# A new order for the layer norm stage: first tile transposed into two PSUM tiles, second tile's statistics begun with the other half

## The chip, the cores and the metric

The kernel runs on one core of a Trainium2 chip. The metric is the device time of one execution in microseconds (us); the time of the kernel before is the median of three runs. PE is the matmul engine, PEld its weight loads, DVE the vector engine, ACT the scalar engine, POOL the general-purpose engine, and SP issues most of the transfers.

## The reference

The input x has 2048 tokens of 512 values. It is normalised per token (`xn = (x - mean) / sqrt(var + eps)`), and two branches read xn; their sum and x are the output.

```python
xn = _layernorm(x)
return x + _A_ref(xn, A_wqkv, A_wo) + _B_ref(xn, B_w_in, B_w_sp, B_b_sp, B_w_out)
# _A_ref: q, k, v = xn @ wqkv, 32 heads of 16; each token attends to itself and
#         7 earlier tokens at a distance of 2, 4 ... 14; then @ wo
# _B_ref: z = gelu(xn @ w_in), 2 x 688 columns; z2 = layernorm(second half)
#         g = w_sp @ z2 + b_sp;  (z1 * g) @ w_out
```

## The kernel before, in words

The 2048 tokens are 16 tiles of 128. A tile has a place `tb` (0 to 3) and a block `j` (0 to 3); its number is `4 * tb + j`, and a block is the four tiles of one `j`. All matmuls need xn with its 512 values along the partitions, so each tile goes through the same chain: load (L167 in halves for the first two tiles of block 0, L175 for the others), statistics on DVE (`bn_stats`, L213 and L217, `bn_aggr`, L220), reciprocal root on ACT (L223) or, for block 3, on POOL (L226, L227), apply in place on DVE (L231), and a transpose into `xnT`. Block 0 and the first two tiles of block 1 are transposed by PE (L238, L248) into a PSUM tile `pt`, which ACT (L242, L252) or DVE (L253) copies to `xnT`; the other ten tiles by a DMA transpose that SP issues (L257).

What follows the chain closely: the q columns of block 0 are multiplied tile by tile as its transposes arrive (`q_tile`, L327, matmuls of 128 columns), the k columns and those of block 1 as matmuls of 512 or 256 columns (`qk_part`, L321), and ACT copies the results out of PSUM (`qk_copy`, L337). Then come the z matmuls of branch B (`zmm`, L263), whose left operands are `xnT` tiles of blocks 1 and 2, and DVE's products q times k (L361).

Five engines have a manual schedule: every engine executes its instructions in the order in which the program writes them, and waits in that order. Up to the first z matmul this order is written out as calls (L597 to L699). After that it is a list of tokens, `ORDER`, that a loop at L724 turns into calls: `z1.3` is the z matmul of tile `j=1, tb=3`, and so on.

PSUM buffers come from two pools: `ps_mm` with three buffers of two banks, `ps_aux` with two of one bank. A tile of a pool waits until the tile that last had the buffer has been read.

Ahead of the first data PE runs ten matmuls on a tile of zeros (`warm_up(10)`), and two short ones between the transposes of the first two tiles and the first q matmul. The second tile of block 0 arrives in two halves, one issued by SP (`h=0`), one by ACT (`h=1`). `ln_stats(i, 2)` reads them in the order 0, 1:

```python
for n in range(2):
    ln_stats(t0[n], 2)
    ln_root(col(t0[n]))
for n in range(2):
    ln_apply(t0[n])
pts = [tr(t0[n]) for n in range(2)]
tr_copy(t0[0], pts[0], 0, 2)
tr_copy(t0[0], pts[0], 2, 4)
tr_copy(t0[1], pts[1], 0, 2)
warm_up(2, 1)
```

Of the kernel before, what the change touches and what calls it, by code (L numbers as in the profile page):

```python
# [7 lines left out]
BF16 = mybir.dt.bfloat16  # L8
F32 = mybir.dt.float32
# [5 lines left out]
P = 128  # L15
# [24 lines left out]
CHUNKS = (1, 1, 1, 1, 1, 1, 1, 1)  # L40
ORDER = """
z1.3 z2.0 z1.2 z2.2 zg1.3 p0.1 zg2.0 zg1.2 q2.2 zg2.2 p0.3 zs2.2 q2.3 p1.2 qc2.2 p1.3 q2.1 qc2.3 p1.0
z1.0 p0.2 qc2.1 w3 z2.1 p0.0 zg1.0 zs1.0 q2.0 p2.2 zg2.1 a1 z2.3 qc2.0 w2 zg2.3 p2.3 halo zs2.0 z3.0 p2.0 z1.1
w0 zg3.0 b1 z0.1 zg1.1 p2.1 zs2.3 X0 a0 zg0.1 z3.2 Xg0 zs1.1 z3.3 a2 zg3.2 z3.1 zs1.2 zg3.3 z0.2 b0 zg3.1 X4
b2 zg0.2 zs3.3 L0 L1 Xg4 q3.1 p3.2 zs3.1 p3.0 Lc0 q3.0 Lc1 p3.1 qc3.1 q3.2 p3.3 qc3.0 zs0.1 a3 z0.3 qc3.2 q3.3
zg0.3 p4.1 zs1.3 p4.0 z0.0 qc3.3 X1 p4.2 zg0.0 zs0.3 X2 p4.3 Xg1 X5 st.0 zs2.1 st.1 a4 Xg2 L2 V6 zs0.2 zs3.2
b3 Xg5 V2 b4 Vc6 zs0.0 p5.3 L3 V5 zs3.0 p5.2 Vc2 V1 st.2 p5.1 Vc5 p5.0 V0 st.3 a5 w4 Lc2 Vc1 V4 st.4 Vc0 w1
N1.1 V3 N2.0 Vc4 N1.0 b5 Lc3 V7 N0.0 Vc3 M0.0 N1.2 M0.1 L5 N0.2 L4 Vc7 N3.3 X6 N0.1 M0.2 N0.3 late X3 N3.1
N1.3 N2.1 G0.0 N2.2 Xg6 N2.3 N3.2 N3.0 G0.1 p7.1 G0.2 M0.3 G0.3 p7.2 G4 p6.0 Gi0 w6 Lc4 p6.3 Xg3 p6.2 E0 p7.3
G3 p6.1 U0 S0.0 p7.0 a6 w9 G1 Gi3 Gi4 S0.1 b6 a7 G2 Gi1 w7 U1 S0.2 b7 S0.3 w5 S0.4 Lc5 R0 L6 L7 G6 Lc6 A0 Gi2  # L50
Lc7 U2 U4 mask T4 U3 M1.0 A1 T2 G7 A2 Gi6 w8 A3 wo1.2 A4 T0 A5 X7 M1.1 Gi7 A6 wo1.3 xr0 G5 A7 Xg7 A8 w10 M1.2
A9 w12 U7 A10 X8 Gi5 A11 X10 T1 A12 G8 Xg10 A13 Xg8 wo1.0 A14 T7 M1.3 A15 G9 Gi8 A16 A17 E1 A18 A19 wo0.2
wo0.3 G10 wo0.1 U6 wo1.1 U5 Gi9 wo0.0 A20 T3 S1.0 S1.1 A21 X9 S1.2 G12 A22 S1.3 Gi10 T5 A23 S1.4 T6 A24 Xg9
w15 A25 X15 A26 Gi12 w14 X12 R1 Xg15 X11 A27 Xg12 w11 A28 O0 Xg11 A29 A30 A31 Or0 O1 A32 A33 A34 Or1 U8 Oh0.0
A35 A36 Oh0.1 Fe0.0 A37 Fe0.1 A38 G14 Fe0.2 Fe0.3 F0.2 F0.0 F0.1 s0.0 A39 s0.1 F0.3 A40 xr1 A41 Oh1.0 w13 A42
U10 Oh1.1 Fe1.0 U9 T8 Gi14 A43 Fe1.1 A44 T10 X13 A45 G11 s0.2 T9 A46 s0.3 F1.0 A47 A48 G13 F1.1 Gi11 s1.1 Xg13
U11 U12 Fe1.2 A49 T12 A50 A51 X14 A52 G15 Xg14 Fe1.3 U14 Gi13 F1.3 F1.2 A53 s1.2 T11 A54 T14 A55 O2 Gi15 s1.0
A56 U15 U13 T15 A57 Or2 xr2 Oh2.0 A58 A59 s1.3 Oh2.1 T13 Fe2.0 Fe2.1 xr3 F2.0 O3 Fe2.2 Fe2.3 F2.2 F2.1 s2.0
s2.2 F2.3 s2.1 s2.3 Or3 Of Oh3.1 end
# [10 lines left out]
def kernel(  # L70
# [98 lines left out]
    def load_wqk(E, s):  # L169
        for kc in range(C):  # L170
            E.dma_start(wqk[:, s, kc], A_wqkv[kc * P:(kc + 1) * P, s * D:(s + 1) * D])

    def load_x(E, j, b0, b1):
        for tb in range(b0, b1):
            E.dma_start(xall[:, j, tb], xblk[j][:, tb])  # L175
# [4 lines left out]
    load_x(A, 0, 2, 4)  # L180
    load_wqk(SP, 0)
    load_x(SP, 1, 0, 2)
    load_wqk(SP, 1)
    load_x(SP, 1, 2, 4)
    load_x(SP, 2, 0, 4)
# [23 lines left out]
    def ln_stats(i, parts=1):  # L209
        j, tb = i % 4, i // 4  # L210
        w = D // parts
        for h in range(parts):
            V.bn_stats(stats[:, i, 6 * h:6 * h + 6], xall[:, j, tb, w * h:w * h + w])  # L213
        ln_agg(i, parts)

    def ln_bn(i):
        V.bn_stats(stats[:, i, 0:6], xall[:, i % 4, i // 4, :])  # L217

    def ln_agg(i, parts=1):
        V.bn_aggr(mv[:, i, :], stats[:, i, 0:6 * parts])  # L220

    def ln_root(sl):
        A.activation(rstd[:, sl], mv[:, sl, 1], ACT.Abs_reciprocal_sqrt, bias=eps_t[:])  # L223

    def ln_root_pool(i):
        G.tensor_tensor(rstd[:, i:i + 1], mv[:, i, 1:2], eps_t[:], ALU.add)  # L226
        G.tensor_tensor(rstd[:, i:i + 1], rstd[:, i:i + 1], mhalf[:], ALU.pow)  # L227

    def ln_apply(i):
        j, tb = i % 4, i // 4  # L230
        V.tensor_scalar(xall[:, j, tb, :], xall[:, j, tb, :], mv[:, i, 0:1], rstd[:, i:i + 1],  # L231
                        ALU.subtract, ALU.mult)

    def tr(i):
        j, tb = i % 4, i // 4
        pt = ps_aux.tile([P, C, P], BF16, name="pt", tag="aux")
        for c in range(C):
            PE.transpose(pt[:, c, :], xall[:, j, tb, c * P:(c + 1) * P], ident[:])  # L238
        return pt

    def tr_copy(i, pt, c0=0, c1=C):
        A.copy(xnT[:, c0:c1, i * P:(i + 1) * P], pt[:, c0:c1, :])  # L242

    def tr2(i):
        j, tb = i % 4, i // 4
        pts = [ps_aux.tile([P, 2, P], BF16, name="pt", tag="aux") for _ in range(2)]
        for c in range(C):
            PE.transpose(pts[c // 2][:, c % 2, :], xall[:, j, tb, c * P:(c + 1) * P], ident[:])  # L248
        return pts

    def tr_copy2(i, pts):
        A.copy(xnT[:, 0:2, i * P:(i + 1) * P], pts[0][:])  # L252
        V.tensor_copy(xnT[:, 2:4, i * P:(i + 1) * P], pts[1][:])  # L253

    def tr_dma(i):
        j, tb = i % 4, i // 4
        SP.dma_start_transpose(xnT[:, :, i * P:(i + 1) * P], xall[:, j, tb, :])  # L257
# [66 lines left out]
    def q_tile(tb, kcs):  # L324
        for kc in kcs:
            for c in range(C):
                PE.matmul(pqs[c // 2][:, c % 2, tb * P:(tb + 1) * P], wqk[:, 0, kc, c:D:C],  # L327
                          xnT[:, kc, 4 * tb * P:(4 * tb + 1) * P], start=(kc == 0 and tb % 2 == 0), stop=(kc == C - 1 and tb % 2 == 1))
# [252 lines left out]
    def blk(j):  # L581
        return [4 * tb + j for tb in range(TB)]

    def col(i):
        return slice(i, i + 1)

    def blk_cols(j):
        return slice(j, NT, 4)

# [4 lines left out]

    t0, i1 = blk(0), blk(1)
    i2, i3 = blk(2), blk(3)
    warm_up(10)  # L597
    for n in range(2):
        ln_stats(t0[n], 2)
        ln_root(col(t0[n]))  # L600
    for n in range(2):
        ln_apply(t0[n])
    pts = [tr(t0[n]) for n in range(2)]
    tr_copy(t0[0], pts[0], 0, 2)
    tr_copy(t0[0], pts[0], 2, 4)
    tr_copy(t0[1], pts[1], 0, 2)
    warm_up(2, 1)
    pqs = [qk_tile() for _ in range(3)]
    ln_stats(t0[2])
    ln_root(col(t0[2]))  # L610
    tr_copy(t0[1], pts[1], 2, 4)
    q_tile(0, (0, 1))
    q_tile(0, (2,))
    q_tile(1, (0, 1))
    q_tile(0, (3,))
    ln_bn(t0[3])
    ln_apply(t0[2])
    ln_agg(t0[3])
    pt2 = tr2(t0[2])
    q_tile(1, (2, 3))  # L620
    ln_root(col(t0[3]))
    tr_copy2(t0[2], pt2)
    ln_apply(t0[3])
    q_tile(2, (0, 1))
    pt3 = tr2(t0[3])
    q_tile(2, (2, 3))
    tr_copy2(t0[3], pt3)
    q_tile(3, (0, 1))
    q_tile(3, (2, 3))
    ln_stats(i1[0])  # L630
    ln_root(col(i1[0]))
    qk_copy(pqs[0], 0, 0)
    ln_stats(i1[1])
    ln_root(col(i1[1]))
    qk_part(pqs[2], 0, 2, 0, 4, (0,))
    ln_apply(i1[0])
    qk_part(pqs[2], 0, 2, 0, 4, (1,), kcs=range(2))
    pt = tr(i1[0])
    qk_part(pqs[2], 0, 2, 0, 4, (1,), kcs=range(2, 4))
    ln_stats(i1[2])  # L640
    qk_copy(pqs[1], 0, 1)
    ln_root(col(i1[2]))
    ln_apply(i1[1])
    tr_copy(i1[0], pt)
    ln_bn(i1[3])
    ln_apply(i1[2])
    tr_dma(i1[2])
    ln_agg(i1[3])
    pq3 = qk_tile()
    qk_part(pq3, 0, 3, 0, 4, (0,), kcs=range(2))  # L650
    pt = tr(i1[1])
    qk_part(pq3, 0, 3, 0, 4, (0,), kcs=range(2, 4))
    tr_copy(i1[1], pt)
    ln_root(col(i1[3]))
    ln_apply(i1[3])
    tr_dma(i1[3])
    load_x(SP, 3, 0, 4)
    qk_part(pq3, 0, 3, 0, 4, (1,))
    qk_copy(pqs[2], 0, 2)
    qk_copy(pq3, 0, 3)  # L660
    for n in range(4):
        ln_stats(i2[n])
    ln_root(slice(2, 7, 4))
    ln_root(slice(10, 15, 4))
    A.preload_act_table_set("gelu_apprx_tanh_and_others")
    table[0] = "gelu"
    for i in i2:
        ln_apply(i)
        tr_dma(i)
    for n in range(3):  # L670
        ln_stats(i3[n])
        ln_root_pool(i3[n])
    ln_apply(i3[0])
    tr_dma(i3[0])
    ln_stats(i3[3])
    ln_root_pool(i3[3])
    for i in i3[1:3]:
        ln_apply(i)
        tr_dma(i)
    pqs = [qk_tile() for _ in range(3)]  # L680
    for c in range(3):
        qk_part(pqs[c], 1, c, 0, 2)
    pa3 = ps_aux.tile([P, 2, 2 * P], F32, name="pa3", tag="aux")
    qk_part(pa3, 1, 3, 0, 2)
    qk_copy(pa3, 1, 3, 0, 2)
    for c in range(3):
# [70 lines left out]
```

## Time and profile before

| | |
|---|---|
| median of 3 runs | 202.04 us (201.27 to 202.22) |
| profiled execution, first to last instruction | 199.94 us |
| what lies around it: median less that span | 2.10 us |
| PE busy | 195.4 us, 98% |
| DVE busy | 184.6 us, 92% |
| ACT busy | 103.9 us, 52% |
| moved by DMA | 25.91 MB, mean 130 GB/s |
| mean granted TensorE clock | 1.000 |

A profile is one execution. A row of its groups or timeline names the line of the kernel, the engine, the operation, the tile written and the tile read; what stands in brackets is the engine's idle time ahead of it and what ended it. The chain of waits is followed back from the last instruction to whatever released each step. [...]

### The profile page before, as it was taken

What the parts mean: (1) busy time and instruction counts of PE and PEld (TensorE: products, weight loads), DVE (VectorE), ACT (ScalarE), POOL (GpSimd) and SP (SyncE); (2) the same over time, 40 slices, a digit from 0 to 9 for tenths busy, and PEclk for the clock granted to TensorE, in tenths of its full rate; (3) what the DMA queues carried; (4) which work ended last, traced back from release to release, by engine and by line L of the source; (5) the groups of instructions that cost most, each with busy time, mean ns of one, the idle gap of its engine ahead of it and who ended that gap; (6) DMA issues with size and microseconds to landing.
All of it is one profiled execution on the core that took longest, in us unless ns stands there. A gap on an engine that the chain in (4) does not pass through costs nothing.

```text
span 199.9 us, 4102 instructions
## 1 busy us (share of the span) xinstructions
PE 195.4 (98%) x1691; PEld 123.9 (62%) x1691; DVE 184.6 (92%) x249; ACT 103.9 (52%) x175; POOL 22.0 (11%) x23
## 2 busy tenths in 40 slices
PE   7899999999999999999999999999999999999994
PEld 2869756665566666666656666666544646664562
DVE  5789899999999999999979999999999999999624
ACT  3586978899899976453431523708402230331400
POOL 3000800699500000000000000000000000000000
DMA  5986548950000096524477999199940297219863
GB/s 160 266 244 163 106 78 240 234 113 3 0 0 3 3 157 115 167 64 100 61 152 161 239 220 192 49 217 180 192 85 0 81 208 169 72 32 127 215 209 105
DMA packets 66562, 25.91 MB, mean 130 GB/s; under 512 B 56496, under 2 KB 66288, under 8 KB 66288
## 3 DMA queue, kind: packets, MB, share of 16 engines
q1 hardware_dynamic: 65824, 25.18, 58.4%
q10 hardware_dynamic: 720, 0.48, 0.8%
q8 instruction: 13, 0.21, 0.4%
q14 instruction: 5, 0.04, 0.1%
HBM read 10.13 MB, written 2.10 MB: 61 GB/s over the span
## 4 chain that ended last, share of the span: by engine, by line
PE 95%; DMA 1%; DVE 1%; SPq 0%; ACT 0%; issue 0%
PE pg L470 37%; PE pz L263 19%; PE pq L321 11%; PE pv L431 7%; PE po L553 7%; PE po L523 6%; PE pa L553 2%; PE pq L327 2%; DMA r_x<-in_A_x_dram 1%; PE pl L381 1%; PE pa L321 1%; PE po L532 1%; PE pb L523 1%; PE pt L238 0%; DVE r_pr L541 0%; DVE stats L213 0%
## 5 line engine op out<-in xcount | busy, mean ns | idle before, releaser
L470 PE MATMUL pg<-z,r_qk 128*128 128x344 bf16 x448 | 66.8, 309 | 0.0
L470 PEld LDWEIGHTS <-r_qk 128*128 128x128 bf16 x448 | 43.8, 98 | 22.0 <-issue 0.4
L445 DVE TENSOR_TENSOR r_pr<-r_x,r_w 128x2048 bf16<-128x2048 bf16 x32 | 38.4, 1220 | 1.3 <-PE pl L381 1.0
L263 PE MATMUL pz<-w_z,xnT 128*128 128x344 bf16 x256 | 39.3, 309 | 0.0
L449 DVE TENSOR_TENSOR r_pr<-r_pr 128x2048 bf16<-128x2048 bf16 x28 | 33.9, 1219 | 0.4
L263 PEld LDWEIGHTS <-xnT 128*128 128x128 bf16 x256 | 25.0, 98 | 13.2 <-issue 0.4
L476 ACT ACTIVATE gs<-pg,b_col 128x688 bf16<-128x688 f32 x16 | 13.2, 834 | 35.4 <-PE pg L470 26.4
L361 DVE TENSOR_TENSOR r_pr<-r_qk 128x2048 bf16<-128x2048 bf16 x24 | 27.9, 1222 | 0.2 <-ACT r_qk L337 0.2
L321 PE MATMUL pq<-xnT,r_w 128*128 128x512 bf16 (+1 forms) x128 | 23.8, 339 | 0.0
L321 PEld LDWEIGHTS <-r_w 128*128 128x128 bf16 x144 | 15.9, 114 | 7.6 <-issue 0.4
L536 ACT CAST r_qk<-po 128x512 bf16<-128x512 f32 x10 | 5.5, 588 | 22.7 <-PE po L553 22.7
L699 POOL CAST b_col<-b 128x16 f32<-128x16 bf16 x1 | 15.7, 15704 | 11.8 <-DMA b<-in_B_b_sp_dram 11.8
L337 ACT CAST r_qk<-pq 128x1024 bf16<-128x1024 f32 x15 | 14.9, 1015 | 2.4 <-PE pq L321 2.3
L312 ACT ACTIVATE r_uz<-pz 128x688 bf16<-128x688 f32 x16 | 11.7, 740 | 6.6 <-PE pz L263 6.5
L523 PE MATMUL po<-r_lg,r_pr 32*128 32x512 bf16 x192 | 14.5, 375 | 0.0
L431 PE MATMUL pv<-xnT,r_w 128*32 128x512 bf16 x256 | 14.2, 379 | 0.0
L553 PEld LDWEIGHTS <-r_uz 128*128 128x128 bf16 x85 | 8.0, 98 | 9.5 <-issue 1.1
L370 DVE TENSOR_TENSOR r_pr<-r_pr 128x4096 bf16<-128x4096 bf16 x6 | 13.7, 2289 | 0.0
L553 PE MATMUL po<-r_w,r_uz 128*128 128x512 bf16 x60 | 13.6, 380 | 0.0
L281 ACT ACTIVATE z<-pz 128x688 bf16<-128x688 f32 x16 | 11.9, 744 | 1.5 <-PE pz L263 1.5
L287 ACT ACTIVATE junk<-z 128x688 bf16<-128x688 bf16 x16 | 12.4, 774 | 0.1
L431 PEld LDWEIGHTS <-r_w 128*32 128x32 bf16 x256 | 9.5, 138 | 4.3
(88 smaller groups left out, 200.3 us busy)
## 6 DMA issues: line engine op xcount, KB each, us to landing
r_lg<-in_A_wo_dram SPq DMA_DIRECT2D x8, 256.0 KB, 4.2
r_x<-in_A_x_dram SPq DMA_DIRECT2D x12, 128.0 KB, 3.0
out_dram<-r_qk SPq DMA_DIRECT2D x12, 128.0 KB, 2.1
r_w<-in_A_wqkv_dram SPq DMA_DIRECT2D x8, 128.0 KB, 3.6
r_qk<-in_A_x_dram SPq DMA_DIRECT2D x8, 128.0 KB, 2.2
w_z<-in_B_w_in_dram SPq DMA_DIRECT2D x4, 172.0 KB, 4.4
w_z<-in_B_w_in_dram SPq DMA_DIRECT2D x1, 688.0 KB, 5.5
r_w<-in_B_w_out_dram SPq DMA_DIRECT2D x1, 640.0 KB, 6.5
```

The costliest lines, as they stand in the source:

```text
L263: PE.matmul(pz[:, hh, 0:FHALF], xnT[:, kc, i * P:(i + 1) * P], wz[:, kc, hh * FHALF:(hh + 1) * FHALF], start=(kc == 0), stop=(kc == C - 1))
L321: PE.matmul(pq[:, cc, p0 * P:(p0 + b1 - b0) * P], wqk[:, sd, kc, c0 + cc:D:C], xv[:, kc, b0:b1, j, :], start=(kc == 0), stop=(kc == C - 1))
L337: cast = A.copy(dst, pq[:, :, p0 * P:(p0 + b1 - b0) * P].rearrange("p c (b t) -> p c b t", b=b1 - b0))
L361: prod = V.tensor_tensor(pr[g % 3][:, c].rearrange("p w b t -> p b w t"), q3.unsqueeze(2).broadcast_to([P, TB, 4, P]), k4, ALU.mult)
L370: V.tensor_tensor(pr[g % 3][:, 0:2], pr[g % 3][:, 0:2], pr[g % 3][:, 2:4], ALU.add)
L431: PE.matmul(pv[32 * tb:32 * tb + 32, dd, :], wv[:, kc, 2 * d2 + dd, :], xnT[:, kc, tb * TBS:(tb + 1) * TBS], start=(kc == 0), stop=(kc == ...
L445: V.tensor_tensor(pw_t[n], vp[:, :, off:off + P], a_sb[:, slot_w(w), ts].unsqueeze(1).broadcast_to([P, DH, P]), ALU.mult)
L449: V.tensor_tensor(pw_t[n] if dst is None else dst, pw_t[n], pw_t[m], ALU.add)
L470: PE.matmul(pg[:, hh, 0:FHALF], wsp[n][:, k, :], z2[:, k, hh * FHALF:(hh + 1) * FHALF], start=(k == 0), stop=(k == NT - 1))
L523: PE.matmul(pc, op[32 * tb:32 * tb + 32, d, o * P:(o + 1) * P], wo_r[32 * tb:32 * tb + 32, d, cs], start=(d == 8), stop=False, tile_positi ...
L553: mm = PE.matmul(pc, uT[:, o % 2, m, tb * P:(tb + 1) * P], wout[:, m, cs], start=False, stop=(m == MCH - 3))
L699: G.tensor_copy(b_col[:], b16[:])
```

## The change

The calls that wrote out the first stage become tokens of a second list, `START`, ahead of `ORDER`; the first tokens of `ORDER` move to its end, and the rest is the same text. The loads are the same transfers in the same order on the same queues; the last block's tiles are loaded in the order 0, 1, 3, 2. In the new order:

- The second tile's statistics read half 1 (ACT's) and then half 0 (SP's): `ls0.1.1 ls0.1.0`.
- The two short warm-up matmuls stand ahead of the first transposes.
- The first tile's four transposes go into two `ps_aux` tiles of two each (`lt0.0.0.2 lt0.0.2.4`), the second tile's into one large tile of `ps_mm` (`lt0.1.0.4.1`).
- The q matmuls run tile 0 to its end, then the first half of tile 1, where before they alternated.
- The third tile's two copies are both ACT's; the fourth tile is transposed after one quarter of the third tile's q matmuls instead of two.
- In block 1 the statistics of tile 3 come ahead of tile 2, and one copy of a whole tile goes to DVE (`lc1.1.0.4.1`).
- In block 2 the statistics of the second tile come first, and the DMA transposes go out as tiles 0, 1, 3, 2. Those of block 3 go out as 3, 0, 2, 1.
- Some of the k matmuls of block 0 stand in another order around the transposes of block 1.

No matmul, activation or statistics is added or removed.

```diff
+START = """
+warm10.4 ls0.0.0 ls0.0.1 la0.0 lr0.0 ls0.1.1 ls0.1.0 la0.1 lr0.1 ln0.0 ln0.1 warm2.1 lt0.0.0.2 lt0.0.2.4 lt0.1.0.4.1 lc0.0.0.2 lc0.0.2.4 lc0.1.0.2 ls0.2 la0.2 lr0.2 lc0.1.2.4 qt0.0 qt0.1 qt0.2 qt0.3 qt1.0 qt1.1 ls0.3 ln0.2 la0.3 lr0.3 lt0.2.0.2 lt0.2.2.4 ln0.3 lc0.2.0.2 lc0.2.2.4 qt1.2 qt1.3 qt2.0 lt0.3.0.2 lc0.3.0.2 lt0.3.2.4 qt2.1 qt2.2 qt2.3 qt3.0 ls1.0 lc0.3.2.4.1 qt3.1 qt3.2 qt3.3 la1.0 lr1.0 c0 ls1.1 la1.1 lr1.1 ln1.0 km2.1.0.2 km2.0.0.4 km2.1.2.4 lt1.0 km3.0.0.2 ls1.3 ls1.2 la1.2 c1 lr1.2 ln1.1 lt1.1 lc1.0.0.4 ln1.2 ld1.2 la1.3 km3.0.2.4 lr1.3 lc1.1.0.4.1 ls2.1 ln1.3 ld1.3 lx3.0.1 lx3.1.2 lx3.3.4 km3.1.0.4 y0.0 c2 c3 ls2.0 la2.0 la2.1 lr2.0.2 ln2.0 lx3.2.3 ld2.0 ls2.2 ls2.3 la2.2 la2.3 lr2.2.2 ln2.1 ln2.3 ld2.1 ld2.3 ls3.0 la3.0 lp3.0 ls3.1 la3.1 lp3.1 ln2.2 ls3.2 ld2.2 la3.2 lp3.2 ls3.3 la3.3 lp3.3 ln3.0 ln3.1 ln3.2 y1.0 y2.0 y3.0 gelu yc3.0 y0.1 yc0 y1.1 y2.1 yc1 y3.1 yc2 yc3.1 p1.1 ln3.3 ld3.3 ld3.0 ld3.2 ld3.1 lv lz lb z1.3 z2.0 z1.2 z2.2 zg1.3 p0.1 zg2.0 zg1.2 q2.2 zg2.2 p0.3 zs2.2 q2.3 p1.2 qc2.2 p1.3 q2.1 qc2.3 p1.0 z1.0 p0.2 qc2.1 w3 z2.1 p0.0 zg1.0 zs1.0 q2.0 p2.2 zg2.1 a1 z2.3 qc2.0 w2 zg2.3 p2.3 halo zs2.0 z3.0 p2.0 z1.1 w0 zg3.0 b1 z0.1 zg1.1 p2.1 zs2.3 X0 a0 zg0.1 z3.2 Xg0 zs1.1 z3.3 a2 zg3.2 z3.1 zs1.2 zg3.3 z0.2 b0 zg3.1 X4 b2 zg0.2 zs3.3
+"""
...
+    def ln_stats(j, tb, h=None):
+        i = 4 * tb + j
+        if h is None:
+            V.bn_stats(stats[:, i, 0:6], xall[:, j, tb, :])
+        else:
+            halves.add(i)
+            V.bn_stats(stats[:, i, 6 * h:6 * h + 6], xall[:, j, tb, 256 * h:256 * h + 256])
...
+    def tr(j, tb, c0=0, c1=C, big=0):
+        if big:
+            pt = ps_mm.tile([P, 16, P], BF16, name="pt", tag="mm")
+        else:
+            pt = ps_aux.tile([P, c1 - c0, P], BF16, name="pt", tag="aux")
+        for c in range(c0, c1):
+            pts[j, tb, c] = pt, c0
+            PE.transpose(pt[:, c - c0, :], xall[:, j, tb, c * P:(c + 1) * P], ident[:])
+
+    def tr_copy(j, tb, c0, c1, on_dve=0):
+        i = 4 * tb + j
+        pt, o = pts[j, tb, c0]
+        (V.tensor_copy if on_dve else A.copy)(xnT[:, c0:c1, i * P:(i + 1) * P], pt[:, c0 - o:c1 - o, :])
...
+    def qk_step(sd, ms, tb, kc):
+        for m in ms:
+            for cc in range(2):
+                PE.matmul(p0[m][:, cc, tb * P:(tb + 1) * P], wqk[:, sd, kc, 2 * (m % 2) + cc:D:C],
+                          xnT[:, kc, 4 * tb * P:(4 * tb + 1) * P], start=(kc == 0 and tb % 2 == 0),
+                          stop=(kc == C - 1 and tb % 2 == 1))
...
+    steps = {"warm": warm_up, "ls": ln_stats, "la": ln_agg, "lr": ln_root, "lp": ln_root_pool, "ln": ln_apply, "lt": tr,
+             "lc": tr_copy, "ld": tr_dma, "qt": q_step, "kt": k_step, "kk": k3_step, "km": k_wide, "qw": q_pair, "kp": k_pair, "nb": ln_shift, "c": c0_copy, "y": y_part, "yt": y_tile, "yc": y_copy,
+             "lx": lambda j, b0, b1: load_x(SP, j, b0, b1), "lw": load_z2, "lv": load_v, "lz": load_z1, "lb": load_b,
...
+    for tok in START.split() + ORDER.split():
```

In a token the first number after the name is the block and the second the tile's place in it (`ls` statistics, `la` aggregate, `lr` and `lp` root on ACT and POOL, `ln` apply, `lt` transposes on PE with the range of the four 128-value pieces, `lc` copy, `ld` DMA transpose, `qt` q matmuls of one tile and one piece, `km` k matmuls of block 0, `y` q and k matmuls of block 1, `c` and `yc` their copies).

## Prediction

> **What bounds the kernel now.** I read the page first: PE is busy for 98% of the span and makes up 95% of the chain that ended last.
>
> ```profile
> PE 195.4 (98%) x1691; PEld 123.9 (62%) x1691; DVE 184.6 (92%) x249; ACT 103.9 (52%) x175; POOL 22.0 (11%) x23
> ...
> PE 95%; DMA 1%; DVE 1%; SPq 0%; ACT 0%; issue 0%
> ```
>
> A busy PE may hide short stalls, so I took the start times of successive matmuls next. Those of 128 columns start 56 ns apart, 512 columns 216 ns, 344 columns 146 ns. From 6.03 us until the last one at 196.91 us only two starts come later than that without a change of form: 0.065 us each, at 8.48 and 9.66 us. So behind 6.03 us there are 0.13 us to win on PE, and everything else must come from starting earlier. The chain of waits up to 30 us, in order of time, shows what sets that start (start, length, what):
>
> ```profile
> 1.25 2.92 DMA r_x<-in_A_x_dram
> 4.17 0.02 issue
> 4.20 0.76 DVE stats L213 x2
> 4.96 0.02 issue
> 4.98 0.22 DVE mv L220
> 5.20 0.02 issue
> 5.23 0.30 ACT rstd L223
> 5.53 0.03 issue
> 5.56 0.42 DVE r_x L231
> 5.98 0.05 issue
> 6.03 0.40 PE pt L238 x4
> 6.42 0.11 PE pwm L592 x2
> 6.53 1.35 PE pq L327 x24
> ```
>
> The end hangs on one transfer: the half of the second token tile that SP issued at 1.25 us and that is whole at 4.17 us. Statistics, aggregate, root, apply and transpose follow without slack. The timeline says the same from the engines' side:
>
> ```profile
> 5.53 0.90 PE L238 MATMUL pt<-ident,r_x 128*128 128x128 bf16 x8 [0.60 <-DVE r_x L231]
> ...
> 5.96 0.92 ACT L242 COPY xnT<-pt 128x256 bf16<-128x256 bf16 x3 [0.44 <-PE pt L238]
> ...
> 7.28 0.40 DVE L231 TENSOR_SCALAR r_x<-r_x,mv,rstd 128x512 bf16<-128x512 bf16 x1
> ```
>
> **Statistics of the second tile.** The landing events of the trace say when each transfer was whole: SP's half at 4.17 us, ACT's half at 3.99 us. The kernel before reads SP's half first, so DVE, which could take a new instruction at about 3.95 us, stands until 4.20. The changed order reads ACT's half at 3.99 + 0.02 = 4.02 us; its successor starts 0.34 us later, at 4.36, when the other half has long landed. The aggregate moves from 4.98 to 4.80 us, **0.18 us earlier**. DVE then runs on without a wait, so apply, root and statistics of the next tiles all move by 0.18: the first apply to 4.93, the second to 5.38, the third tile's apply from 7.28 to 7.10 us.
>
> **The first tile in two PSUM tiles.** Its first copy now waits for two transposes instead of four. A transpose shows 0.219 us from start to end and a copy starts 0.037 us behind (5.922 to 5.959), so two fewer starts bring the copy 0.11 us forward: with the apply's 0.18 it starts at 5.67 and ends at 6.04. The two short warm-up matmuls, 0.11 us in the chain, move ahead of the transposes into PE's idle time. The first q matmul needs the second tile's transposes issued (apply ends 5.79, they start at 5.85, four times 0.056: 6.08) and the copy (6.04 + 0.05), so it starts at 6.09 instead of 6.38, 0.29 earlier. But that lead isn't kept. Twenty-four q matmuls take 1.34 us (to 7.43; the fourth quarter of the q weights, whole at 6.80 us, holds them back by about 0.09 to 7.52), and then the third tile's transposes wait for its apply: 7.10 + 0.40 + 0.06 = 7.56 instead of 7.74. So 0.11 of the 0.29 is lost to a new wait, and **the split itself is worth nothing here**; its cover is DVE's chain.
>
> **Tiles three and four.** Tile three's second copy moves from DVE to ACT (0.29 and 0.37 us there), which lets DVE apply tile four at 7.96 instead of 8.38. The q matmuls on tile three still wait for the copy after its transposes (8.30 for 8.48). The other wait of 0.065 us, at 9.66, goes: tile four's transposes now stand four q matmuls earlier, its copy ends at 9.21, and PE comes at 9.41. **Gain 0.065 us.**
>
> **Blocks one to three.** PE is then 0.25 us early at its first 512-column matmul (10.31 for 10.55). What could stop it:
> - The second tile of block one is transposed at 12.69; its apply ends, by the DVE rows (landing of the last quarter of the block at 10.78, two statistics of 0.68 and 0.66, aggregate 0.18, apply 0.38), at 12.58. That leaves 0.05 us after the 0.06 that the transpose lags. This cover is thin, because the tile that lands last is now measured first.
> - One 128x512 copy leaves ACT (0.59 us) for DVE, ahead of a matmul that needs it at 14.2 us; by two copies of 0.29 it ends near 13.7. On ACT the two later q copies end near 14.4 and 15.4; PE needs them at 15.1 and 15.9 (now 0.28 and 0.23 us to spare).
> - SP issues the same loads in the same order. Its transposes of block one follow the applies: 13.15 and 14.60 us, now 13.62 and 15.03. What is queued behind moves by 0.43: the eight transposes from 18.38 to about 17.95.
> - The wait on POOL's root (0.44 us of DVE before its second product) sits behind 24 us and costs PE nothing.
>
> No instruction is added or removed on PE, so behind this stage the 0.25 us stay. DVE, which also starts its products about 0.25 earlier (22.85 for 23.12), keeps its distance.
>
> **Sum.** 0.18 + 0.065 = 0.245 us off the profiled execution's 199.94 us span: 199.69. The runs shown have a median of 202.04 us, 2.10 above that span (launch and end, and the spread of executions); less 0.25, **201.8 us**. The unknown costs, from both sides: if the third apply did not hold PE, the gain would be 0.36; if SP's half lands first, the 0.18 is gone.
>
> **Rivals.**
> 1. *No gain.* The lead of ACT's half is 0.18 us in one execution, on DMA engines that are 80% busy from 2 to 4 us and 92% from 4 to 6. If it flips, DVE waits for the later half in the changed order as it does now, and 0.07 us remain; a last quarter of block one late by 0.2 us costs 0.15. Then 202.0 us.
> 2. *Slower: a stall at the z matmuls (L263) of block two.* The transposes of block two now go out as tiles 0, 1, 3, 2, and PE needs tile 2 before tile 3. At 1.3 us apiece tile 2 is issued at 21.86 and lands at 24.33 us (fourth place: 22.29 to 24.76 before); PE comes at 24.94 - 0.25 = 24.70. It decides from a landing 0.36 us late. The row that speaks for it: of the sixteen landing events of the transfer now in fourth place, fifteen lie by 24.76 and one at 25.86, 1.10 late, beside an instruction fetch at 24.50; PE then needed it at 25.96. A repeat would land at 25.43: stall 0.73, net +0.5, so 202.5 us. The next one was late by 2.12 us (27.33, 29.45) beside a fetch of 1.47 us; that would stall 1.75 and give 203.5 us. Against it: such fetches are few, eighteen in the span by the page's rows and four of them between 11 and 30 us, and the place is earlier by 0.43 us.
>
> ```profile
> q8 instruction: 13, 0.21, 0.4%
> q14 instruction: 5, 0.04, 0.1%
> ```
>
> 3. *Faster by over 1 us*, if executions that I have not seen hold stalls in this stage that the new order avoids (tile 3 of block two, with 0.11 us to spare in the profile, now goes third): about 200.9 us.
>
> [...]
>
> That the change doesn't do what it says I rule out: in the program, each of the first three copies has its own wait on PE, and the second tile's first statistics wait on ACT's transfer.
>
> **Chances.** Forecast 0.57, no gain 0.15, stall of a good half microsecond 0.13, stall of 1.5 us or more 0.08, faster by over 1 us 0.07. About 0.5%, 1.0 us, is what a measurement of this kernel tells from no change (its runs spread over 201.27 to 202.22). The first three cases lie within it: faster 0.07, same 0.85, slower 0.08. The range goes from the fastest run less the largest gain (201.27 - 0.36 = 200.9) to the slowest with the smaller stall and some of the flip (202.22 + 0.5 + 0.1 = 202.8).
>
> **What would show it.** Right: second tile's statistics start near 4.02 us, first q matmul near 6.1, third tile's transposes near 7.56, the first 512-column matmul near 10.31, the z matmuls of block two without a gap, span 199.7. Wrong: the statistics start at 4.2 again (rival 1), or matmuls on block two's tile 2 start behind a gap near 24.7 (rival 2), or PE has gaps near 12.7.

## The result, and the profile after

The changed kernel takes **202.71 us** (median of 11 runs, 201.69 to 203.33) where the kernel before takes 201.68 us (median of 11 runs, 201.27 to 202.22). The ratio is 1.0042 with a 95% interval of 1.0027 to 1.0057: slower, by less than 0.5%, where 0.1% faster was forecast.

The runs of the changed kernel lie in two groups. With the twelve of the first experiment there are 23: nine from 201.35 to 202.06 us (mean 201.79) and fourteen from 202.45 to 203.33 (mean 202.87). So two questions stand: what the 1.1 us are that fourteen of 23 runs pay, and why the other nine are no faster than before.

The profiled execution took 201.77 us, so it belongs to the lower group: span 200.1 us, 0.1 more than the 199.94 of before (unrounded, 200.05). From its page, busy time and the chain by engine, with matmuls now on L259 (z), L317 and L325 (q, k), transposes on L244:

```profile
PE 196.1 (98%) x1691; PEld 124.3 (62%) x1691; DVE 184.7 (92%) x249; ACT 103.9 (52%) x175; POOL 5.6 (3%) x23
...
PE 98%; DVE 0%; ACT 0%; issue 0%
```

The chain of waits (start, length, what) no longer begins with a transfer:

```profile
1.04 4.66 PE pwm L642 x12
5.71 0.23 PE pt L244 x2
5.93 0.02 issue
5.95 0.38 ACT xnT L249
6.33 0.04 issue
6.38 1.69 PE pq L325 x24
8.07 0.22 PE pt L244 x4
...
10.81 1.73 PE pq L317 x8
```

On DVE the times came out as forecast: in its timeline the second tile's statistics start at 3.96 us (4.20 before) and the third tile's apply at 7.10, as forecast. But the first q matmul starts at 6.38 as before, not at 6.09, because PE itself was late: the clock rose only at 5.78 us in this execution, the transposes went 107 ns apart, and the twelve warm-up matmuls ahead of them filled PE's time. Then the 24 q matmuls take 0.19 us longer than before, because they wait for the third and the fourth quarter of the q weights (whole, by the last of their landing events, at 6.86 and 7.16 us; 6.41 and 6.80 before), and 0.08 of that comes back at tile four. So the first 512-column matmul starts at 10.65 us (10.55 before), and what follows keeps that distance to the end. PE's timeline shows the four z products without a break, before and after (24.70 was forecast for the fourth; it starts at 25.03):

```profile
21.44 4.83 PE L263 MATMUL pz<-w_z,xnT 128*128 128x344 bf16 x32
```

```profile
21.53 4.83 PE L259 MATMUL pz<-w_z,xnT 128*128 128x344 bf16 x32
```

So this one execution of the lower group shows why it isn't faster than before. It holds nothing of the upper group; that took another profile.

### The profile page after: what moved, and what is told of

It reads as the page before. It is cut to its first block, busy times and chain, and to the rows that moved or that the text cites. A ratio compares the mean times of both kernels' runs of the same rounds, so it can differ in the third digit from the quotient of the medians.

```text
span 200.1 us, 4105 instructions
## 1 busy us (share of the span) xinstructions
PE 196.1 (98%) x1691; PEld 124.3 (62%) x1691; DVE 184.7 (92%) x249; ACT 103.9 (52%) x175; POOL 5.6 (3%) x23
## 4 chain that ended last, share of the span: by engine, by line
PE 98%; DVE 0%; ACT 0%; issue 0%
PE pg L529 37%; PE pz L259 19%; PE pq L317 11%; PE pv L490 7%; PE po L612 7%; PE po L582 6%; PE pwm L642 2%; PE pq L325 2%; PE pa L612 2%; PE pl L440 1%; PE pa L317 1%; PE po L591 1%; PE pb L582 1%; PE pt L244 1%; DVE r_pr L600 0%; ACT xnT L249 0%
## 5 line engine op out<-in xcount | busy, mean ns | idle before, releaser
L259 PE MATMUL pz<-w_z,xnT 128*128 128x344 bf16 x256 | 39.3, 310 | 0.0
L259 PEld LDWEIGHTS <-xnT 128*128 128x128 bf16 x256 | 24.9, 98 | 13.2 <-issue 0.4
L317 PE MATMUL pq<-xnT,r_w 128*128 128x512 bf16 (+1 forms) x128 | 23.8, 340 | 0.0
L317 PEld LDWEIGHTS <-r_w 128*128 128x128 bf16 x144 | 15.9, 114 | 7.6 <-issue 0.4
L582 PEld LDWEIGHTS <-r_pr 32*128 32x128 bf16 x272 | 7.5, 93 | 6.7 <-issue 1.0
```

The lines of the kernel that those rows point to most:

```text
L259: PE.matmul(pz[:, hh, 0:FHALF], xnT[:, kc, i * P:(i + 1) * P], wz[:, kc, hh * FHALF:(hh + 1) * FHALF], start=(kc == 0), stop=(kc == C - 1))
L317: PE.matmul(pq[:, cc, p0 * P:(p0 + b1 - b0) * P], wqk[:, sd, kc, c0 + cc:D:C], xv[:, kc, b0:b1, j, :], start=(kc == 0), stop=(kc == C - 1))
L582: PE.matmul(pc, op[32 * tb:32 * tb + 32, d, o * P:(o + 1) * P], wo_r[32 * tb:32 * tb + 32, d, cs], start=(d == 8), stop=False, tile_positi ...
```

## The experiments

**e1: the changed kernel again**, for a second profile.

> The changed kernel once more, for a second profile and more times. Its eleven times lie in two groups, 201.7 to 201.9 us (three, the profiled one among them) and 202.4 to 203.3 us (eight). Late landing (the second rival of the prediction): in the upper group the DMA transpose of block two's tile 2, now fourth, lands about 1 us late, and a profile of that group shows a gap of 0.7 to 1.1 us on PE near 24.8 us. Late clock: in the upper group PE's clock comes up later than the 5.8 us of the profile shown, and a profile of that group shows q matmuls 107 ns apart instead of 56 for some microseconds behind 6 us, and no gap at 24.8. Both expect a ratio near 1.004.

Measured: 202.27 us (12 runs), ratio 1.0031 (1.0013 to 1.0049). Its profiled execution took 203.19 us, one of the upper group, although the clock rose early, at 4.28 us. A late clock is therefore not what the upper group pays for. PE's timeline, and the chain that led to the broken place:

```profile
21.77 3.66 PE L259 MATMUL pz<-w_z,xnT 128*128 128x344 bf16 x24
26.46 1.34 PE L259 MATMUL pz<-w_z,xnT 128*128 128x344 bf16 x8 [1.03 <-DMA xnT<-r_x]
```

```profile
22.92 0.09 DVE r_x L233
23.02 3.40 DMA xnT<-r_x
26.42 0.05 issue
26.46 1.34 PE pz L259 x8
```

Eight of the 32 z matmuls, those on tile 2 of block two, stand behind a DMA transpose issued at 23.02 us that took 3.40 us to land. Start to start, PE loses 1.20 us there: about 0.93 because the landing is that much later than the 2.47 us that a transpose in time takes, 0.22 because the transpose was issued too late for PE even so, and 0.05 from landing to start. That is the second rival's place.

**e2 to e4: which edit makes it.** e2 puts only block two's transposes back in the order 0, 1, 2, 3, e3 only the two short warm-ups; e4 gives the kernel before only the new order of transposes.

```diff
# e2, in START
-ln2.1 ln2.3 ld2.1 ld2.3
+ln2.1 ln2.2 ld2.1 ld2.2
...
-ln2.2 ls3.2 ld2.2
+ln2.3 ls3.2 ld2.3
# e3, in START
-ln0.1 warm2.1 lt0.0.0.2
+ln0.1 lt0.0.0.2
...
-lc0.1.0.2 ls0.2
+lc0.1.0.2 warm2.1 ls0.2
# e4, in the kernel before
-    for i in i2:
+    for i in (i2[0], i2[1], i2[3], i2[2]):
         ln_apply(i)
         tr_dma(i)
```

> The changed kernel with the DMA transposes of block two (and the applies ahead of them) in the order 0, 1, 2, 3 again. Late landing: PE gets tile 2 from the third place, 1.3 us earlier, the upper group goes, the ratio falls to about 0.999. Late clock: the first 10 us are untouched, so the ratio stays near 1.004 and the two groups stay.

> The changed kernel with the two short warm-up matmuls back between the transposes and the q matmuls. Late landing: nothing changes, ratio near 1.004 (the two matmuls cost 0.1 us at most). Late clock: if the place of these two matmuls decides when the clock comes up, the upper group goes or shrinks and the ratio falls towards 1.000.

> The kernel before with one part of the change alone: DMA transposes of block two in the order 0, 1, 3, 2. Late landing: the same upper group appears, ratio 1.002 to 1.005. Late clock: same as before within 0.1%.

| | median us | ratio (95%) | PE gap at the fourth z product |
|---|---|---|---|
| e2 | 201.87 (201.79 to 202.31) | 1.0013 (1.0005 to 1.0022) | none |
| e3 | 202.95 (202.55 to 203.49) | 1.0063 (1.0049 to 1.0077) | 0.91 us |
| e4 | 202.38 (202.27 to 202.48) | 1.0034 (1.0021 to 1.0047) | 0.67 us |

e2 removes the upper group (its clock rose at 6.98 us, the latest of all), e4 makes it out of the kernel before. PE's timeline of e2, then of e4:

```profile
21.62 4.83 PE L259 MATMUL pz<-w_z,xnT 128*128 128x344 bf16 x32
```

```profile
21.41 3.66 PE L263 MATMUL pz<-w_z,xnT 128*128 128x344 bf16 x24
25.58 1.34 PE L263 MATMUL pz<-w_z,xnT 128*128 128x344 bf16 x8 [0.50 <-DMA xnT<-r_x]
```

The bracket gives less than the gap from start to start (0.50 for 0.67 us in e4), since a matmul's end is modelled. All five runs of e4 lie between 202.27 and 202.48 us. e3 shows that the place of the warm-ups isn't the cause. Its ratio lies above e1's: all six of its runs are in the upper group, of e1's six of twelve, and no row shows why.

**e5 to e8: where the lead of 0.25 us went.** On e2, whose profile has no stall: e5 puts the old order of the first 24 q matmuls back, e6 the old order of the second tile's halves, e7 the first tile's transposes in one PSUM tile. e8 gives the kernel before the new order of q matmuls.

```diff
# e5
-qt0.0 qt0.1 qt0.2 qt0.3 qt1.0 qt1.1
+qt0.0 qt0.1 qt0.2 qt1.0 qt1.1 qt0.3
# e6
-ls0.1.1 ls0.1.0
+ls0.1.0 ls0.1.1
# e7
-lt0.0.0.2 lt0.0.2.4
+lt0.0.0.4
# e8, in the kernel before
-    q_tile(1, (0, 1))
     q_tile(0, (3,))
+    q_tile(1, (0, 1))
```

> The base is e2 (the changed kernel with block two's transposes in the order 0, 1, 2, 3). The first 24 q matmuls go in the old order again: the fourth quarter of the weights is first needed by the 21st of them, not by the 13th. Theory (the new q order exposes the landing of the weights): the third tile's transposes start at the end of that tile's apply, near 7.55 to 7.6 us, instead of 7.80 to 8.07, the first 512-column matmul near 10.3 to 10.4 instead of 10.54 to 10.82; the ratio falls from 1.0013 to 0.9985 to 0.9995. Rival (the place where PE waits doesn't matter, because the applies on DVE or a cold clock set the third tile): third tile still behind 7.8, ratio 1.001 to 1.002.

> e2 with the second tile's halves read in the old order, SP's half first. By the prediction's first step this loses 0.18 us, ratio 1.0022. By what the four profiles since show (SP's half whole 0.17 us before ACT's, and both there before DVE asks) it loses nothing and may gain up to 0.1 us: ratio 1.001 to 1.0015, statistics of the second tile without a wait.

> e2 with the first tile's four transposes in one PSUM tile again, the two copies as they are. Prediction's step (the split is worth nothing): first copy 0.1 us later, first q matmul up to 0.1 later, third tile's transposes no later than in e2, ratio within 0.0005 of e2's 1.0013. Rival (the lead of the q matmuls is kept because PE waits for no apply there): 0.1 us slower, ratio 1.0018 or more.

> The kernel before, with one edit: the fourth quarter's four matmuls on the first tile go ahead of the second tile's eight, as in the changed kernel. Theory (exposed weights): third tile's transposes start 0.7 us behind the landing of that quarter, 7.6 to 8.0 us for 7.74, so 0 to 0.3 us lost, ratio 1.0005 to 1.0015. Rival (the weights are hidden): ratio 1.0000 within 0.0005.

| | median us | ratio (95%) |
|---|---|---|
| e5 | 201.87 | 1.0010 (0.9998 to 1.0022) |
| e6 | 201.79 | 1.0002 (0.9993 to 1.0012) |
| e7 | 201.96 | 1.0010 (0.9998 to 1.0021) |
| e8 | 201.89 | 1.0001 (0.9993 to 1.0010) |

By the times no single edit is worth 0.2 us beyond the intervals, and e5's theory missed its ratio. (One of e5's twelve runs took 202.60 us, and one of the 35 of the kernel before beside it 202.47; neither was profiled, so not every time above 202.4 us need be the stall.) e5's profile shows why. The third tile's transposes start at 7.56 us and the first 512-column matmul at 10.31, both as forecast. Then its chain shows a wait that the lead uncovered:

```profile
7.68 3.39 DMA r_x<-in_A_x_dram
11.07 0.02 issue
11.10 1.30 DVE stats L205 x2
12.40 0.02 issue
12.42 0.18 DVE mv L212
12.60 0.31 DVE r_x L233
12.91 0.05 issue
12.96 0.40 PE pt L244 x4
```

The last quarter of block one was whole at 11.07 us. The changed order measures that tile first (`ls1.3 ls1.2`), and the second tile's apply stands behind both statistics: PE's transposes start 0.27 us late, and the z matmuls start at 21.47 us, for 21.44 before. This is the cover that the prediction called thin.

The wait for weights is real in some executions: the view of the weight loads' waits has a row (us in total, times, longest), in e6 and then in e1. In both it is the third quarter of the q weights, whole at 7.18 and 7.02 us, and the ninth q matmul starts 0.05 us behind it. The ninth matmul needs this quarter in the old order of q matmuls too, so e5's edit, which only moves the need for the fourth quarter, can't remove this wait:

```profile
PEld L325 <- DMA r_w<-in_A_wqkv_dram: 0.5, 1, 0.5
```

```profile
PEld L325 <- DMA r_w<-in_A_wqkv_dram: 0.6, 1, 0.6
```

e8's theory fell: there the clock rose at 6.29 us, the chain starts with PE's own warm-ups, and q starts too late to meet the weights (whole at 6.37 and 6.86 us, needed at 6.83 and 7.05).

```profile
1.04 4.45 PE pwm L592 x10
5.49 0.85 PE pt L238 x8
```

e7's profile can't weigh the split: both halves of the second tile were late, and all waited for DVE's row.

```profile
4.72 0.75 DVE L208 BATCH_NORM_STATS2 stats<-r_x 128x6 f32<-128x256 bf16 x2 [0.83 <-DMA r_x<-in_A_x_dram]
```

The marks of the stage side by side (us; weights: landing of the third and the fourth quarter of the q weights; the forecast's first z is before's less 0.25):

| | clock rises | first q | weights | third tile | first 512 columns | first z |
|---|---|---|---|---|---|---|
| before | not recorded | 6.38 | 6.41, 6.80 | 7.74 | 10.55 | 21.44 |
| forecast | | 6.09 | (third not named), 6.80 | 7.56 | 10.31 | 21.19 |
| after | 5.78 | 6.38 | 6.86, 7.16 | 7.90 | 10.65 | 21.53 |
| e1 | 4.28 | 6.05 | 7.02, 7.33 | 8.07 | 10.82 | 21.77 |
| e5 | not recorded | 5.99 | 6.60, 6.95 | 7.56 | 10.31 | 21.47 |
| e6 | 5.59 | 6.28 | 7.18, 7.48 | 8.23 | 10.97 | 21.86 |
| e8 | 6.29 | 6.38 | 6.37, 6.86 | 7.72 | 10.52 | 21.41 |
| e9 | 6.07 | 6.38 | 7.06, 7.41 | 8.03 | 10.77 | 21.66 |
| e10 | 4.55 | 5.94 | 6.15, 6.75 | 7.40 | 10.16 | 21.23 |

**e9 to e11: the lead with the thin cover mended, with and without the new order of transposes.** e9 is e5 with block one's statistics in the old order, e10 is e9 with block two's transposes as 0, 1, 3, 2 again (e2's edit reversed), e11 is e9 with both edits of the title undone (those of e6 and e7).

```diff
# e9
-ls1.3 ls1.2 la1.2 c1 lr1.2 ln1.1 lt1.1 lc1.0.0.4 ln1.2
+ls1.2 la1.2 c1 lr1.2 ln1.1 lt1.1 lc1.0.0.4 ls1.3 ln1.2
```

> e5 with block one's statistics in the old order: the third tile of the block is measured first and the second tile's apply no longer stands behind the statistics of the tile that lands last. Theory (in e5 the lead of 0.25 us at the first 512-column matmul went into a wait of 0.27 us for the second tile's apply, behind that late landing): no gap near 12.5 us, PE 0.2 to 0.3 us ahead of the kernel before at the z matmuls (21.2 us), ratio 0.9985 to 0.9995. Rival (a later wait takes the lead as well): the gap is gone, the ratio stays at 1.000 or above and another gap shows between 13 and 27 us.

> e9 with the one edit of the changed kernel put in again: block two's transposes in the order 0, 1, 3, 2. Theory (that order costs a wait at the z matmuls of tile 2 of 0.7 to 1.2 us in most executions): ratio 0.002 to 0.005 above e9's, gap near 24.5 us in the profile. Rival (the wait came only with the delays of the stage before, which e9 lacks, so the transposes go out earlier and are in time): ratio within 0.001 of e9's, no gap.

> e9 with both edits of the title taken out: the first tile in one PSUM tile again and the second tile's halves in the old order. Theory (neither is worth anything in the median): ratio within 0.0007 of e9's. Rival (the two are worth the 0.1 to 0.2 us that the prediction worked out for the half order, or for the split's cover): ratio 0.0007 to 0.0015 above e9's.

| | median us | ratio (95%) |
|---|---|---|
| e9 | 201.70 (201.41 to 201.93) | 0.9997 (0.9987 to 1.0007) |
| e10 | 202.65 (201.27 to 202.96) | 1.0033 (1.0014 to 1.0052) |
| e11 | 201.82 (201.39 to 202.03) | 1.0004 (0.9993 to 1.0014) |

e9 has no gap near 12.5 us and has the lowest ratio of all versions, but it isn't measurably faster than before; its profiled execution lost 0.28 us ahead of the ninth q matmul, to the third quarter of the weights (whole at 7.06 us). e11 against e9 shows nothing for the title's two edits within the intervals. e10 against e9 is the cleanest price of the transposes' order: 0.0036 of 201.65 us, **0.73 us** (by the two intervals, some 0.3 to 1.2), and the two groups are back (three runs up to 201.70 us, nine from 202.17). Its profile had the lead of 0.2 us and a gap of 0.94:

```profile
21.23 3.66 PE L259 MATMUL pz<-w_z,xnT 128*128 128x344 bf16 x24
25.67 1.34 PE L259 MATMUL pz<-w_z,xnT 128*128 128x344 bf16 x8 [0.78 <-DMA xnT<-r_x]
```

**e12: who reads the late tile.** The changed kernel with its transposes as they are; tiles 2 and 3 of block two change places in the lists of z products, gelus and squares.

```diff
-z1.3 z2.0 z1.2 z2.2
+z1.3 z2.0 z1.2 z2.3
...
-z2.3 qc2.0
+z2.2 qc2.0
```

> The changed kernel with its DMA transposes as they are (0, 1, 3, 2); only PE's order, with the gelu and square behind it, is changed: tile 3 of block two takes the place of tile 2 at the fourth z product, so that PE meets the transpose in third place there and the one in fourth place only at the 512-column matmuls 1.17 us later. Theory (the loss is the wait for the fourth transpose, whose last landing is late in part of the executions): the runs of 202.4 us and above go, ratio 1.000 to 1.002; a late landing leaves at most 0.1 to 0.5 us at the 512-column matmuls. Rival (the order 0, 1, 3, 2 itself delays the queue or DVE, whoever reads the tile): ratio stays at 1.003 to 1.004.

Measured: 201.91 us (201.59 to 202.33), ratio 1.0010 (1.0001 to 1.0019). The runs of 202.4 and above are gone, although the fourth transpose landed late in its profile too (3.27 us after its issue). PE's timeline has no break:

```profile
21.60 4.83 PE L259 MATMUL pz<-w_z,xnT 128*128 128x344 bf16 x32
```

So neither the order of the queue nor DVE costs the time by itself. It is the wait of the first reader for the transpose in fourth place.

## Why the prediction was wrong, step by step

- **The step that failed: the sum put the wait for block two's tile 2 at nothing.** The second rival happened. Its place and its wait (PE stands for one transpose's late landing) were in the prediction, but it had a chance of 0.13, argued from few instruction fetches in the span. The runs showed the wait in 14 of 23 of the changed kernel, by their times; the gaps in four profiles are 0.67, 0.91, 0.94 and 1.20 us, for the 0.73 of the prediction. A count of fetches over 200 us says nothing on whether the one at this place recurs. It does, as the table of the last section shows: in fourteen profiles the fourth transpose was late in ten. The row in before's profile (one landing 1.10 us late) was the usual case, and the kernel before was covered against it: it reads the fourth tile only at the 512-column matmuls at 26.11 us, 1.17 us behind the place where the changed kernel reads it.
- **The margin of 0.36 us, and some luck in the price.** It was worked out from an issue at 21.86 us, with the whole row of eight transposes 0.43 us earlier. In after the row starts only 0.12 us earlier (18.26 for 18.38), and the fourth issue came between 21.94 and 23.21 us in the profiles with the new stage (22.18 in after). In the four profiles with a gap the margin was 0.20 (e4), 0.09 (e10), -0.04 (e3) and -0.22 us (e1). The landing, on the other hand, was 0.82 to 0.99 us late there, not 1.10. So 0.73 us came near because one error made up for the other; with the margin kept, these gaps would have been 0.5 to 0.7 us.
- **0.18 us from the half order: a draw of one execution.** Before's profile had SP's half at 4.17 us. In twelve of the other thirteen profiles both halves were whole by 3.77 us, before DVE had finished the first tile's statistics, whichever order was used. e7, at 4.70, is the other. In after the second tile's statistics start early, as forecast, but not for the order of the halves: both were whole by 3.58 us. e6 takes the edit out and loses nothing.
- **The q matmuls at 6.09 us** hold only where the clock rises early (5.90 us in e3, 5.94 in e10, 6.05 in e1, with rises at 4.12, 4.55 and 4.28); where it rose at 5.78 us or later they start at 6.38, as before. An early rise is not enough: in e11, without the title's two edits and with the first tile whole 0.23 us later than in before, they start at 6.33 after a rise at 4.61. The prediction took the transposes' 56 ns from a profile and didn't ask when the clock rises.
- **The weights' fourth quarter at 6.80 us, 0.09 us lost: mostly the wrong quarter, and too small.** The third quarter, which the prediction didn't look at, landed between 6.15 and 7.18 us over fourteen profiles (6.41 in before). It held PE first in six of them, for 0.09 (after) to 0.57 us (e1); each time the ninth q matmul started 0.05 us behind its landing. The fourth landed between 6.63 and 7.48 us and cost up to 0.41 us (e12). By the times e5 against e2 and e8 against before, which move the fourth quarter's need alone, show no difference.
- **0.065 us at tile four: right.** From the third tile's transposes to the first 512-column matmul it is 2.74 us in after, 2.82 in before and 2.81 in e8.
- **The split is worth nothing: not contradicted** (e7, e11).
- **"What could stop it", the second tile of block one: right as a place, and thinner than said.** The terms listed there add up to 12.68 us, not 12.58. In e5 the transposes start 1.88 us behind the landing, which from 10.78 us gives 12.66, 0.03 ahead of the 12.69 and not 0.05. With the lead kept and a landing 0.29 us later, e5 lost 0.27 us there.
- **The base.** The forecast time of 201.8 us is 0.25 off a median of three runs, 202.04. With eleven runs the kernel before has 201.68, and the same 0.25 off it would be 201.43.

Of the loss, the stall is the larger part: 14 of 23 runs times 1.08 us is 0.66 us, where the ratios of both series (1.0042, 1.0031) say 0.74 us on the mean. The rest is under 0.1 us, about what the lower group lies above the kernel before. The gain that was forecast, 0.25 us, did not come in either group. Three things with spreads of half a microsecond or more (second tile whole at 3.58 us in after and 4.70 in e7, third quarter of the weights from 6.15 to 7.18, clock up from 4.12 to 6.98) set the start of this stage, and an edit that shortens one is worth only the distance to the next.

## What to carry to other kernels

A late landing seen once in a profile, and hidden there, is a warning about whoever is moved next to it: before moving a consumer, look for the latest of a transfer's landing events and keep its cover, or give the place to a consumer that comes later. A gain of 0.2 us read from one arrival time should be checked against a second execution of the same kernel. Where runs fall in two groups, profile one of each.

## What the runs showed of the hardware

**The fourth DMA transpose of the row.** Third place: 2.49 to 2.50 us from issue to last landing in all fourteen profiles. Fourth place:

| | fourth issued, us | fetch begins behind issue | landed behind issue | late landings of 16 |
|---|---|---|---|---|
| after | 22.18 | 2.20 | 2.48 | 0 |
| e2, e6, e11 | 21.94 to 22.49 | 2.21 to 2.48 | 2.47 | 0 |
| before | 22.29 | 2.21 | 3.57 | 1 |
| e3, e4, e5, e8, e12 | 22.24 to 22.50 | 1.84 to 1.97 | 3.27 to 3.32 | 1 |
| e1, e7, e9, e10 | 22.17 to 23.21 | 1.81 to 1.90 | 3.40 to 3.46 | 16 |

The fetch is the one of queue q14. Where it begins within 2 us of the issue, the transpose is late, nine times of nine; from 2.2 us on, once in five. The last late event comes 0.85 to 1.05 us behind the fetch's recorded end in the six profiles with one late event, 1.24 to 1.27 us in the four with sixteen. A fetch nearby is not enough: the last transpose of the row had one begin 0.17 to 0.94 us behind its issue in nine profiles, and landed within 2.55 us in all of them. All this is a correlation over profiles; no run moved the fetch by itself, so it stays open whether it holds the landing back. In three of the four with all sixteen events late the DMA engines moved at most 8 GB/s in any slice of 0.2 us behind the fourth transpose's own packets: from 25.0 to 26.4 us in e1, 24.8 to 26.2 in e9 and 24.2 to 25.8 in e10. The busy row of the DMA engines in e10, from 20 to 28 us in such slices, has the fourth transpose's packets up to 24.2 us and the fetch behind them, and then at most 4 GB/s until 25.8, yet the transpose was whole only at 25.63:

```profile
DMA  9500899200499500099930000000049950008999
```

**The clock** rose between 4.12 and 6.98 us in the eleven profiles that record it, with PE busy from 1.04 us in the same way. In after, where it rose at 5.78 us, the 128-column matmuls start 107 ns apart until then, and 56 ns apart afterwards.
